# Seven inner products for each of three products: layer 1 of the last four batches of an attention and feed-forward kernel

## The chip, the cores and the metric

The kernel runs on one core of a Trainium2 chip. The metric is the device time of one execution in microseconds (us); lower is better. The engines are named as the profile names them: PE is TensorE's matmul, PEld its weight load, DVE is VectorE, ACT is ScalarE, POOL is GpSimd, and SP is the engine that issues most DMAs.

## What is computed

Eight batches of eight heads go through an attention whose queries are averaged in pairs: `softmax(scale * q_pool @ k.T) @ v`. This gives `x`, 576 rows of 512 numbers for each batch. Then, per batch, 128 rows are chosen by a gate score and only these pass a two-layer network:

```python
scores = np.einsum('bsd,d->bs', x, w_gate)
top_idx = np.argpartition(-scores[b], capacity)[:capacity]   # capacity 128
xe = x[b, top_idx]
h = np.maximum(xe @ w1, 0.0)                                 # w1 512 x 1024
ye = h @ w2                                                  # w2 1024 x 512
g = 1.0 / (1.0 + np.exp(-scores[b, top_idx]))
out[b, top_idx] = x[b, top_idx] + g[:, None] * ye
```

All of it is float32. The change concerns `xe @ w1` for batches 4 to 7 and the order of the work around it.

## The kernel before

The attention fills the first 568 us. It runs pair of heads by pair of heads, two batch halves in flight, with every matmul on 64 x 64 quarters of the array. Routing (choosing the 128 rows of a batch) is a Python generator that is advanced a piece at a time between the other work.

`ending` (L1381) then does the network for all eight batches, four at a time. The 128 chosen rows of four batches are 512 rows, and each of the two matrix products is made as a 2 x 2 block product in seven block products instead of eight. For layer 1 the four input blocks are named a11, a12, a21, a22 (two batches by half of the 512 inputs each), the weight blocks b11 to b22 (half of the inputs by half of the 1024 hidden units), and there are four sums of inputs s1 to s4 (`input_sums`, L1249, on POOL) and of weights t1 to t4 (made earlier, in the tile `tw`). `first_layer` (L1300) makes the products in the order a11 b11, a12 b21, s2 t2, s1 t1, s4 b22, s3 t3, a22 t4, which the text calls P1, P2, P4, P3, P6, P5 and P7. Each is a `first_product` (L1265): eight matmuls of a 128 x 128 weight block against 256 columns; each shows as two records in the profile. ACT copies the first to SBUF (`u`), and DVE adds the others onto running sums, 128 x 1024 at a time (L1298 is the shared helper `add`). When a hidden quarter c11, c12, c22 or c21 is complete, ACT applies the ReLU in place (L1309).

Layer 2 is the same scheme for two batches at a time. `second_of` (L1353) makes seven `second_product`s (L1280) of four matmuls with 256 columns each, in the order 1, 2, 7, 3, 4, 5, 6; ACT copies four of them and DVE adds the rest, then scales by the gate and adds to `xe` (L1293). Its input sums are `four_sums` (L1344) on DVE. `scattered` writes the finished rows back with an indirect DMA from POOL (L1240). The two last batches go through a layer 2 written out at the end of `ending`.

So the stages in time are: layer 1 of batches 0 to 3, layer 2 of batches 0 and 1, of 2 and 3, layer 1 of batches 4 to 7, layer 2 of 4 and 5, of 6 and 7. Between the products stand two other pieces of work: the routing of batches 6 and 7, advanced by `pieces` (L1389) at fixed counts (the tuple `behind`), and a check that no softmax sum is out of range: `counted` (L1505, two DVE passes over 576 columns into the tile `low`) and `outside` (L1522, one tiny matmul on `low` and three tiny DVE operations). In the kernel before these two stand after two and after four products of the second layer 1.

The schedule is manual: each engine executes its instructions in the order in which the program emits them. Every matmul result goes to a tile from `banks` (L1063); the pool has four tiles of two banks each, so that a product waits for a tile until its last reader on DVE or ACT is done.

Of the kernel before, what the change touches and what calls it, by code (L numbers as in the profile page):

```python
# [540 lines left out]
class _Plain:  # L541
# [704 lines left out]
            oob_is_err=False,  # L1246
        )

    def input_sums(self, a, s):  # L1249

        a11, a12, a21, a22 = a
        s1, s2, s3, s4 = s
        add, subtract = ALU.add, ALU.subtract
        for to, x, y, op in (
            (s1, a21, a22, add), (s2, s1, a11, subtract), (s3, a11, a21, subtract), (s4, a12, s2, subtract)
        ):
            self.nc.gpsimd.tensor_tensor(out=to, in0=x, in1=y, op=op)  # L1257

    def lines_of(self, room):
        return room.rearrange("p (c n) -> p c n", n=P)  # L1260
# [36 lines left out]
    def add(self, to, x, y):  # L1297
        self.nc.vector.tensor_tensor(out=to, in0=x, in1=y, op=ALU.add)  # L1298
# [54 lines left out]
    def second_of(self, tokens, a, s, y):  # L1353

        copy, add = self.nc.scalar.copy, self.add
        half, w = self.Dm // 2, tokens[0]["w"]
        y1, y2, y7, y3, y4 = (y[0:w, i * half : (i + 1) * half] for i in range(5))
        to = [token["xe"][0:w, i * half : (i + 1) * half] for token in tokens for i in range(2)]
        one, two = tokens
        products = self.second_layer(a, s, (1, 2, 7, 3, 4, 5, 6))  # L1360
        for part in (y1, y2, y7):
            copy(part, next(products))
            yield
        copy(y3, next(products))
        add(y2, y2, y1)
        self.scaled(to[0], y2, one, to[0])
        yield
        add(y4, y1, next(products))
        add(y3, y3, y4)
        add(y4, y4, y7)  # L1370
        yield
        ps = next(products)
        add(y4, y4, ps)
        add(y7, y3, ps)
        yield
        add(y3, y3, next(products))
        for of, at, token in ((y3, to[1], one), (y4, to[2], two), (y7, to[3], two)):
            self.scaled(at, of, token, at)
        yield

    def ending(self, halves, old):  # L1381

        nc, half, copy = self.nc, self.Dm // 2, self.nc.scalar.copy
        last = halves[-1]["pair"]
        w = self.tokens[0]["w"]
        n = self.NFC // 2 * 2 * P
        done, behind = 2, (3, 4, 5, 9, 10, 11, 12, 13, 18, 19, 21, 22, 27)

        def pieces(unit, n=None, of=1):  # L1389
            nonlocal done  # L1390
            for i, _ in enumerate(unit):
                for _ in range(of):
                    if done in behind:
                        next(waiting)
                    done += 1
                if i + 1 == n:
                    break

        def exponents_room():
            return self.row(self.work.tile([P, self.NG, G, 2, self.HALF], F32, name="p"))  # L1400

        def values_room():
            return self.row(self.load.tile([P, 2, self.NC, self.D], F32, name="v_sb", bufs=2))

        def sums_room():
            return self.row(self.work.tile([P, G, 2 * self.HALF], F32, name="acc"))

        def first(i):
            x, y = (self.tokens[4 * i + 2 * j]["turned"] for j in range(2))
            a = [t[:, :, k * self.ND // 2 : (k + 1) * self.ND // 2, 0:w] for t in (x, y) for k in range(2)]  # L1410
            c = [self.hidden_of(rooms[i][:, k * n : (k + 1) * n], w) for k in range(4)]
            m = [self.hidden_of(room[:, 4 * n : 5 * n], w) for room in rooms]
            return a, c, self.first_layer(a, inputs, c, m)

        def second(i, j, c):
            a = [c[2 * j + k][:, :, t, :] for t in range(2) for k in range(2)]
            s = self.lines_in(rooms[1 - i][:, 2 * j * n : 2 * (j + 1) * n], self.NFC // 2, w, 4)
            return self.tokens[4 * i + 2 * j : 4 * i + 2 * j + 2], a, s

        self.early = values_room()[:, 0 : 2 * self.Dm]  # L1420
        rooms, acc = [exponents_room()], [sums_room(), sums_room()]
        inputs = [acc[0][:, i * 2 * half : (i + 1) * 2 * half] for i in range(3)]
        inputs.append(self.load.tile([P, self.S], F32, name="kT")[:, 0 : 2 * half])
        inputs = [room.rearrange("p (t c n) -> p t c n", t=2, n=P)[:, :, :, 0:w] for room in inputs]

        self.gated(halves[-3])
        next(old)
        self.weighted(halves[-1])
        self.drained(halves[-1])
        self.multiplied(halves[-2])  # L1430
        rooms.append(exponents_room())
        a, c, layer = first(0)
        self.input_sums(a, inputs)
        self.multiplied(halves[-1])
        self.scored(halves[-3])
        self.gated(halves[-2])
        self.late = values_room()
        next(old)
        next(layer)
        self.normalized(last)  # L1440
        self.gated(halves[-1])
        self.scored(halves[-1])
        _, new, _ = self.routing.pop()
# [12 lines left out]
        self.scattered(x[0])  # L1456
        pieces(self.second_of(*y, acc[1]))
        a, c, layer = first(1)
        self.input_sums(a, inputs)
        self.scattered(y[0])  # L1460

        pieces(layer, 2)
        low = self.counted()
        pieces(layer, 2)
        outside = self.outside(low)
        pieces(layer, 1)
        x, y = second(1, 0, c), second(1, 1, c)
        self.four_sums(*x[1:])
        pieces(layer)
        layer = self.second_of(*x, acc[1])  # L1470
        pieces(layer, 3)
        self.four_sums(*y[1:])
        pieces(layer)
        self.scattered(x[0])

        (six, seven), c, s = y
        to = [token["xe"][0:w, i * half : (i + 1) * half] for token in (six, seven) for i in range(2)]
        y1, y3, y4 = (acc[1][0:w, i * half : (i + 1) * half] for i in range(3))
        found = nc.values_load(outside[0:1, 0:1])
        E = mybir.EngineType  # L1480
        self.tc.mark_branch_hint_location("again", found, [E.PE, E.DVE, E.Pool, E.Activation, E.SP])
# [212 lines left out]
```

## Time and profile before

| what | us |
|---|---|
| median of three runs (672.95 to 673.77) | 673.27 |
| the profiled execution's own time | 673.65 |
| its span in the profile | 671.9 |
| PE busy | 665.1 (99%) |
| DVE busy | 565.2 (84%) |
| POOL busy | 499.8 (74%) |
| ACT busy | 441.2 (66%) |
| layer 1 of batches 4 to 7 on PE | 617.40 to 641.89 |
| layer 2 of batches 4 and 5 on PE | 641.89 to 653.97 |

The span begins with the first instruction of the program that was recorded and ends with the last; the time of the same execution is 1.75 us longer. A group's line gives busy time and the mean duration of one instruction; on DVE and ACT durations of neighbours overlap by some 80 ns, so the step from one start to the next is shorter than a duration. A timeline line gives the start in us, the time until the last of its merged instructions ended, and how many there were.

### The profile page before, as it was taken

What the parts mean: (1) busy time and instruction counts of PE and PEld (TensorE: products, weight loads), DVE (VectorE), ACT (ScalarE), POOL (GpSimd) and SP (SyncE); (2) the same over time, 40 slices, a digit from 0 to 9 for tenths busy, and PEclk for the clock granted to TensorE, in tenths of its full rate; (3) what the DMA queues carried; (4) which work ended last, traced back from release to release, by engine and by line L of the source; (5) the groups of instructions that cost most, each with busy time, mean ns of one, the idle gap of its engine ahead of it and who ended that gap; (6) DMA issues with size and microseconds to landing.
All of it is one profiled execution on the core that took longest, in us unless ns stands there. A gap on an engine that the chain in (4) does not pass through costs nothing.

```text
span 671.9 us, 22869 instructions
## 1 busy us (share of the span) xinstructions
PE 665.1 (99%) x9715; PEld 438.4 (65%) x9715; DVE 565.2 (84%) x811; ACT 441.2 (66%) x959; POOL 499.8 (74%) x465
## 2 busy tenths in 40 slices
PE   9999999999999999999999999999999999999996
PEld 6656666666666666666666666656666666888885
DVE  3878999998999987998899888988898899596463
ACT  5677778777777777778777777777777874221120
POOL 5788888889888988899888978898889877302302
PEclk9999999999999999999999999999999999999999
DMA  8989989868886788859866879588958845303001
GB/s 164 169 178 194 216 173 189 150 113 179 159 154 117 122 163 153 166 105 177 170 117 130 170 137 149 127 160 146 156 112 163 153 139 151 73 16 105 33 2 66
DMA packets 391048, 92.68 MB, mean 138 GB/s; under 512 B 371608, under 2 KB 376088, under 8 KB 390936
## 3 DMA queue, kind: packets, MB, share of 16 engines
q1 hardware_dynamic: 389496, 86.73, 67.1%
q0 software_dynamic: 1280, 4.20, 1.7%
q8 instruction: 78, 1.28, 0.8%
q14 instruction: 34, 0.28, 0.2%
q10 hardware_dynamic: 160, 0.20, 0.1%
HBM read 75.30 MB, written 15.79 MB: 136 GB/s over the span
## 4 chain that ended last, share of the span: by engine, by line
PE 92%; issue 5%; DMA 2%; POOL 1%; DVE 0%; POOLq 0%
PE ps L878 42%; PE ps L896 42%; PE ps L1285 4%; PE ps L1271 4%; DMA out_dram<-xe,index 1%; PE ps L623 1%; DMA out_dram<-v_sb,index 0%; POOL acc L1257 0%; POOL out_dram L1240 0%; PE ps L844 0%; DVE xe L1293 0%; POOL kT L1257 0%; DVE v_sb L1215 0%; PE ps L830 0%; DVE acc L1298 0%
## 5 line engine op out<-in xcount | busy, mean ns | idle before, releaser
L885 ACT ACTIVATE p<-ps 128x576 f32<-128x576 f32 x576 | 320.5, 699 | 2.2 <-PE ps L878 1.9
L917 POOL TENSOR_TENSOR acc<-p 128x576 f32<-128x576 f32 x192 | 283.0, 1501 | 38.3 <-ACT p L885 36.9
L878 PE MATMUL ps<-qT,kT 64*64 64x288 f32 x4608 | 292.0, 403 | 0.0
L896 PE MATMUL ps<-p,v_sb 64*64 64x288 f32 x4608 | 290.9, 403 | 0.0
L878 PEld LDWEIGHTS ps<-qT,kT 64*64 64x64 f32 x4608 | 174.1, 133 | 105.5 <-ACT p L885 13.4
L896 PEld LDWEIGHTS ps<-p,v_sb 64*64 64x64 f32 x4608 | 173.0, 133 | 106.6 <-ACT p L885 14.7
L922 DVE TRANSPOSE_TENSOR_REDUCE fold<-p 128x54 f32<-128x1728 f32 x64 | 126.3, 1974 | 44.3 <-ACT p L885 44.2
L904 ACT COPY two<-ps 128x576 f32<-128x576 f32 x64 | 40.8, 638 | 133.5 <-PE ps L896 131.6
L922 DVE TRANSPOSE_TENSOR_REDUCE fold<-acc 128x54 f32<-128x1728 f32 x64 | 124.5, 1945 | 3.7 <-POOL acc L917 3.5
L906 POOL TENSOR_TENSOR av<-two 128x288 f32<-128x288 f32 x64 | 51.3, 801 | 39.9 <-ACT two L904 39.0
L766 DVE STREAM_TRANSPOSE kT<-kb 128x1152 f32<-128x1152 f32 x31 | 73.9, 2385 | 0.0
L985 POOL TENSOR_TENSOR prod<-avb,w_gate 128x288 f32<-128x288 f32 x64 | 51.5, 805 | 0.0
L1116 DVE TENSOR_SCALAR_CACHE_REDUCE pick<-line 128x127 f32<-128x127 f32 (+4 forms) x80 | 45.2, 564 | 3.4 <-DMA line<-gate_lines 1.2
L763 POOL TENSOR_TENSOR qp<-qb 128x576 f32<-128x576 f32 (+1 forms) x32 | 43.9, 1373 | 5.5 <-DMA qb<-in_q_dram 3.9
L962 ACT ACTIVATE sums<-total,tiny 32x18 f32<-32x18 f32 x124 | 38.2, 308 | 1.9
L1240 POOL DMA_INDIRECT out_dram<-xe,index x7 | 6.9, 992 | 38.7 <-DVE xe L1293 28.2
L1021 POOL TENSOR_TENSOR x<-avb,rec 128x576 f32<-128x576 f32 x30 | 34.8, 1161 | 0.0
L1309 ACT ACTIVATE p<-p 128x1024 f32<-128x1024 f32 x8 | 8.5, 1058 | 39.0 <-DVE p L1298 33.5
L975 DVE STREAM_TRANSPOSE avb<-av 128x288 f32<-128x288 f32 x64 | 28.3, 442 | 3.8 <-POOL av L906 3.8
L1043 DVE TENSOR_REDUCE red<-prod 128x9 f32<-128x288 f32 x64 | 27.8, 435 | 2.7 <-POOL prod L985 2.7
L947 ACT COPY groups<-sum 32x36 f32<-32x36 f32 x124 | 27.2, 219 | 1.6
L1298 DVE TENSOR_TENSOR p<-p,ps 128x1024 f32<-128x1024 f32 x14 | 16.9, 1216 | 11.9 <-PE ps L1271 11.8
(103 smaller groups left out, 420.7 us busy)
## 6 DMA issues: line engine op xcount, KB each, us to landing
kb<-in_k_dram SPq DMA_DIRECT2D x124, 144.0 KB, 4.7
qb<-in_q_dram SPq DMA_DIRECT2D x124, 144.0 KB, 4.5
v_sb<-in_v_dram SPq DMA_DIRECT2D x31, 576.0 KB, 5.1
out_dram<-x SPq DMA_DIRECT2D x128, 72.0 KB, 5.0
lines<-row_rank SPq DMA_DIRECT2D x8, 640.0 KB, 4.2
w<-in_moe_w_dram SPq DMA_DIRECT2D x8, 512.0 KB, 4.7
line<-gate_lines SPq DMA_DIRECT2D x8, 351.5 KB
tw<-tw SPq DMA_DIRECT2D x4, 512.0 KB, 5.7
```

The source lines that it names most:

```text
L763: nc.gpsimd.tensor_tensor(out=qp[:, of, :], in0=pair["q"][:, of, 0, :], in1=pair["q"][:, of, 1, :], op=ALU.add)
L766: nc.vector.transpose(kT.rearrange("p (c i g) -> p c g i", c=self.NC, i=BLK), pair["k"].rearrange("p (g c) d -> p c g d", c=self.NC),)
L878: nc.tensor.matmul(sc[keys, j, 0:n], lhsT=pair["kT"][rows, c * P + keys.start : c * P + keys.stop], rhs=pair["qT"][rows, qs], start=True, ...
L885: nc.scalar.activation(p[:, c // G, c % G, :, :], sc[:, :, 0:n], AF.Exp, scale=self.scale)
L896: nc.tensor.matmul(av[j * self.D : (j + 1) * self.D, e, 0:n], lhsT=half["pair"]["v"][keys, j, c, :], rhs=half["p"][keys, c // G, c % G, j, :],
L904: nc.scalar.copy(two[:, :, :], av[:, :, 0:n])
L906: nc.gpsimd.tensor_tensor(out=half["av"][:, :], in0=two[:, 0, :], in1=two[:, 1, :], op=ALU.add)
L917: nc.gpsimd.tensor_tensor(out=acc[:, u, :], in0=units[:, 0, u, :], in1=units[:, 1, u, :], op=ALU.add)
L922: nc.vector.tensor_reduce(fold[:, a, :], of.rearrange("p u (m d) -> p (u m) d", d=BLK), AX.X, ALU.add, apply_transpose=True,)
L962: self.nc.scalar.activation(tot[rows, :], pair["total"][:, j * self.QB : (j + 1) * self.QB], AF.Identity, bias=self.tiny[0:BLK, 0:1],)
L985: self.nc.gpsimd.tensor_tensor(out=pair["prod"][:, ns, :], in0=pair["avb"][:, ns, :], in1=self.w_gate[:, hp : hp + 1, :].broadcast_to([P, ...
L1116: nc.vector.tensor_scalar(out=cmp[0:rows, 0 : part.stop - part.start], in0=near[0:rows, part], scalar1=sc[0:rows, t : t + 1], scalar2=None ...
```

## The change

Four things are changed.

First, in layer 1 of batches 4 to 7 three of the seven products (P2, P6 and P7) are no longer eight matmuls over 256 columns. Each is divided once more into 2 x 2 blocks: the two batches of a block are taken singly (128 columns each), the contraction is split into its two 128-row chunks, the 512 hidden units into two times 256. An inner product is two matmuls of a 128 x 128 weight block against 128 columns, and seven of them replace the eight matmuls. They lie in halves of six banks (three tiles, taken together). ACT copies the first, and DVE makes seven adds of 128 x 256. P2's result is made in `c11` and P1 is added to it afterwards (`rest`); P6 is made in `u`; P7 is made in `c21`; then `rest` adds `u` to `c12` and `v` to `c21`.

Second, the inner sums are made on POOL: twelve weight sums of 128 x 256 (`inner_weights`, two at each step of `pieces` from the first layer 1 on, into six rooms that the attention leaves), and for each of the three products four input sums of 128 x 128 (`inner_inputs`).

Third, the ReLU of c22, c12 and c21 moves behind P7. The order of layer 2 in `second_of` becomes 1, 5, 2, 7, 3, 4, 6 with other accumulators, in all three calls of it.

Fourth, `counted` and `outside` move into the layer 2 of batches 4 and 5: `counted` after its third product, `outside` after its fourth. The first input sum that layer 2 needs is made between P6 and P5, the other three after P7, and the scatter of batches 2 and 3 is emitted after layer 1.

```diff
+    def inner_weights(self, operands):
+        rooms = self.quarter_rooms()
+        n = self.F // 4
+        for operand in operands:
...
+            for i in range(4):
...
+                self.nc.gpsimd.tensor_tensor(out=to, in0=x, in1=y, op=ALU.subtract)
+                t.append(to)
+                yield
+
+    def inner_product(self, tile, k, i, of, by):
+        to = tile[:, k, 2 * i * P : 2 * (i + 1) * P].rearrange("p (f n) -> p f n", n=P)[:, :, 0 : of.shape[1]]
+        for f in range(2):
+            self.nc.tensor.matmul(to[:, f, :], lhsT=by[:, f * P : (f + 1) * P], rhs=of, start=True, stop=True)
+        return to
+
+    def inner_layer(self, m, to, temps):
...
+        x, y, z = self.banks(), self.banks(), self.banks()
+        u, v, r = temps
+        self.nc.scalar.copy(u, product(x, 0, 0, a11, b11))
+        add(r, u, product(x, 1, 0, s2, t2))
+        add(c11, u, product(y, 0, 0, a12, b21))
+        add(v, r, product(y, 1, 0, s1, t1))
+        ps = product(z, 0, 0, s3, t3)
+        add(c22, v, ps)
+        add(r, r, ps)
+        add(c12, v, product(z, 1, 0, s4, b22))
+        add(c21, r, product(x, 0, 1, a22, t4))
...
+            def layer():
+                copy(across(u), product(a[0], self.quarter(1, 0, 0)))
+                yield
+                self.inner_layer(two, c11, temps[0])
+                rest(c11, u)
+                relu(c11)
+                yield
+                add(across(v), across(u), product(s2, t2))
+                yield
+                add(across(c12), across(v), product(s1, t1))
+                yield
+                self.inner_layer(six, u, temps[1])
+                self.four_sums(*x[1:], slice(2, 3))
+                yield
+                ps = product(s3, t3)
+                add(across(v), across(v), ps)
+                add(across(c22), across(c12), ps)
+                yield
+                self.inner_layer(seven, c21, temps[0])
+                relu(c22)
+                rest(c12, u)
+                relu(c12)
+                rest(c21, v)
+                relu(c21)
+                yield
...
-        products = self.second_layer(a, s, (1, 2, 7, 3, 4, 5, 6))
-        for part in (y1, y2, y7):
-            copy(part, next(products))
-            yield
-        copy(y3, next(products))
-        add(y2, y2, y1)
+        products = self.second_layer(a, s, (1, 5, 2, 7, 3, 4, 6))
+        copy(y1, next(products))
+        yield
+        copy(y5, next(products))
+        yield
+        add(y2, y1, next(products))
         self.scaled(to[0], y2, one, to[0])
         yield
+        add(y2, y5, next(products))
+        yield
+        copy(y3, next(products))
+        yield
         add(y4, y1, next(products))
+        add(y2, y2, y4)
         add(y3, y3, y4)
-        add(y4, y4, y7)
-        yield
-        ps = next(products)
-        add(y4, y4, ps)
-        add(y7, y3, ps)
+        add(y5, y5, y3)
...
+                    for _ in range(2):
+                        next(weights, None)
...
+        self.inner_inputs(operands[0])
         pieces(self.second_of(*y, acc[1]))
-        a, c, layer = first(1)
         self.input_sums(a, inputs)
+        for operand in operands[1:]:
+            self.inner_inputs(operand)
+        c, x, layer = split(a)
+        pieces(layer)
+        self.four_sums(*x[1:], slice(0, 2))
+        self.four_sums(*x[1:], slice(3, 4))
         self.scattered(y[0])
-
-        pieces(layer, 2)
-        low = self.counted()
-        pieces(layer, 2)
-        outside = self.outside(low)
-        pieces(layer, 1)
-        x, y = second(1, 0, c), second(1, 1, c)
-        self.four_sums(*x[1:])
-        pieces(layer)
+        y = second(1, 1, c)
         layer = self.second_of(*x, acc[1])
         pieces(layer, 3)
+        low = self.counted()
+        pieces(layer, 1)
+        outside = self.outside(low)
         self.four_sums(*y[1:])
         pieces(layer)
         self.scattered(x[0])
```

More of the change, by code (lines that the diff above doesn't have):

```diff
@@ L1247, in written, with input_sums @@
         )
-    def input_sums(self, a, s):
+    def input_sums(self, a, s, which=slice(0, 4)):
         a11, a12, a21, a22 = a
@@ L1253, in input_sums, with quarter_rooms @@
         add, subtract = ALU.add, ALU.subtract
-        for to, x, y, op in (
-            (s1, a21, a22, add), (s2, s1, a11, subtract), (s3, a11, a21, subtract), (s4, a12, s2, subtract)
-        ):
+        steps = (s1, a21, a22, add), (s2, s1, a11, subtract), (s3, a11, a21, subtract), (s4, a12, s2, subtract)
+        for to, x, y, op in steps[which]:
             self.nc.gpsimd.tensor_tensor(out=to, in0=x, in1=y, op=op)
+    def quarter_rooms(self):
+        load, work = self.load, self.work
+        yield load.tile([P, self.QB, BLK], F32, name="qp", bufs=1)
+        for _ in range(2):
+            yield load.tile([P, self.Sp], F32, name="qT")
+        yield work.tile([P, self.QB, BLK], F32, name="prod", bufs=1)
+        for name in ("avb", "avb"):
+            yield work.tile([P, self.QB, BLK], F32, name=name)
@@ new lines, in inner_weights @@
+    def inner_weights(self, operands):
+        rooms = self.quarter_rooms()
+        n = self.F // 4
+        for operand in operands:
+            t = operand["t"] = []
+            b11, b12, b21, b22 = (operand["b"][:, k, j * n : (j + 1) * n] for k in range(2) for j in range(2))
+            for i in range(4):
+                if i % 2 == 0:
+                    room = next(rooms)
+                    room = self.row(room) if len(room.shape) > 2 else room
+                to = room[:, i % 2 * n : (i % 2 + 1) * n]
+                x, y = ((b12, b11), (b22, t[0] if t else None), (b22, b12), (b21, t[1] if i == 3 else None))[i]
+                self.nc.gpsimd.tensor_tensor(out=to, in0=x, in1=y, op=ALU.subtract)
+                t.append(to)
+                yield
@@ new lines, in inner_inputs @@
+    def inner_inputs(self, operand):
+        room, w = operand["room"], operand["a"].shape[3]
+        a = [operand["a"][:, i, j, :] for i in range(2) for j in range(2)]
+        operand["s"] = [room[:, i * P : i * P + w] for i in range(4)]
+        self.input_sums(a, operand["s"])
+    def inner_product(self, tile, k, i, of, by):
[3 more added lines that the diff above has]
+        return to
@@ new lines, in inner_layer @@
+    def inner_layer(self, m, to, temps):
+        n = self.F // 4
+        product, add = self.inner_product, self.add
+        a11, a12, _, a22 = (m["a"][:, k, j, :] for k in range(2) for j in range(2))
+        b11, _, b21, b22 = (m["b"][:, k, j * n : (j + 1) * n] for k in range(2) for j in range(2))
+        (s1, s2, s3, s4), (t1, t2, t3, t4) = m["s"], m["t"]
+        c11, c12, c21, c22 = (to[:, 2 * i : 2 * i + 2, :] for i in range(4))
+        x, y, z = self.banks(), self.banks(), self.banks()
[9 more added lines that the diff above has]
+        add(c21, r, product(x, 0, 1, a22, t4))
@@ L1356, in second_of @@
         half, w = self.Dm // 2, tokens[0]["w"]
-        y1, y2, y7, y3, y4 = (y[0:w, i * half : (i + 1) * half] for i in range(5))
+        y1, y2, y5, y3, y4 = (y[0:w, i * half : (i + 1) * half] for i in range(5))
         to = [token["xe"][0:w, i * half : (i + 1) * half] for token in tokens for i in range(2)]
         one, two = tokens
-        products = self.second_layer(a, s, (1, 2, 7, 3, 4, 5, 6))
-        for part in (y1, y2, y7):
-            copy(part, next(products))
-            yield
-        copy(y3, next(products))
-        add(y2, y2, y1)
+        products = self.second_layer(a, s, (1, 5, 2, 7, 3, 4, 6))
[4 more added lines that the diff above has]
+        add(y2, y1, next(products))
         self.scaled(to[0], y2, one, to[0])
         yield
+        add(y2, y5, next(products))
+        yield
+        copy(y3, next(products))
+        yield
         add(y4, y1, next(products))
+        add(y2, y2, y4)
         add(y3, y3, y4)
-        add(y4, y4, y7)
-        yield
-        ps = next(products)
-        add(y4, y4, ps)
-        add(y7, y3, ps)
+        add(y5, y5, y3)
         yield
         add(y3, y3, next(products))
-        for of, at, token in ((y3, to[1], one), (y4, to[2], two), (y7, to[3], two)):
+        for of, at, token in ((y3, to[1], one), (y2, to[2], two), (y5, to[3], two)):
             self.scaled(at, of, token, at)
@@ L1394, in pieces @@
                         next(waiting)
+                    for _ in range(2):
+                        next(weights, None)
                     done += 1
@@ L1406, in sums_room, with halves_of @@
             return self.row(self.work.tile([P, G, 2 * self.HALF], F32, name="acc"))
[L1408 to L1411, printed above, removed]
+        def halves_of(turned):
+            k = self.ND // 2
+            return turned[:, :, 0:k, 0:w], turned[:, :, k:, 0:w]
@@ L1412, in first, with lines, across @@
+        def first():
+            a = [half_of for token in self.tokens[0 : self.B // 2 : 2] for half_of in halves_of(token["turned"])]
+            c = [self.hidden_of(rooms[0][:, k * n : (k + 1) * n], w) for k in range(4)]
             m = [self.hidden_of(room[:, 4 * n : 5 * n], w) for room in rooms]
             return a, c, self.first_layer(a, inputs, c, m)
+        def lines(room):
+            return self.lines_of(room)[:, :, 0:w]
+        def across(room):
+            return room.rearrange("p (t f) n -> p f t n", t=2)
@@ new lines, in rest, with relu, split @@
+        def rest(to, x):
+            self.add(to, to, x)
+        def relu(to):
+            nc.scalar.activation(to, to, AF.Relu)
+        def split(a):
+            u, v = (lines(room[:, 4 * n : 5 * n]) for room in rooms)
+            c11, c12, c21, c22 = c = [lines(rooms[1][:, k * n : (k + 1) * n]) for k in range(4)]
+            temps = [
+                [lines(rooms[0][:, k : k + half]) for k in range(2 * n + 3 * i * half, 2 * n + 3 * (i + 1) * half, half)]
+                for i in range(2)
+            ]
+            two, six, seven = operands
+            s1, s2, s3, s4 = inputs
+            t1, t2, t3, _ = (self.summed(1, i) for i in range(4))
+            x, product, add = second(1, 0, c), self.first_product, self.add
+            def layer():
[23 more added lines that the diff above has]
+                yield
+            return c, x, layer()
@@ L1415, in second @@
         def second(i, j, c):
-            a = [c[2 * j + k][:, :, t, :] for t in range(2) for k in range(2)]
+            if i == 0:
+                a = [c[2 * j + k][:, :, t, :] for t in range(2) for k in range(2)]
+            else:
+                a = [c[2 * j + k][:, 4 * t : 4 * t + 4, :] for t in range(2) for k in range(2)]
             s = self.lines_in(rooms[1 - i][:, 2 * j * n : 2 * (j + 1) * n], self.NFC // 2, w, 4)
@@ L1431, in ending @@
         rooms.append(exponents_room())
-        a, c, layer = first(0)
+        a, c, layer = first()
         self.input_sums(a, inputs)
@@ L1442, in ending @@
         self.scored(halves[-1])
+        operands = [
+            {"b": b, "room": rooms[0][:, k * n // 2 : (k + 1) * n // 2]}
+            for b, k in ((self.quarter(1, 1, 0), 1), (self.quarter(1, 1, 1), 2), (self.summed(1, 3), 3))
+        ]
+        weights = self.inner_weights(operands)
         _, new, _ = self.routing.pop()
@@ L1456, in ending @@
         self.scattered(x[0])
+        a = [half_of for token in self.tokens[self.B // 2 :: 2] for half_of in halves_of(token["turned"])]
+        for operand, of in zip(operands, (a[1], inputs[3], a[3])):
+            operand["a"] = of
+        self.inner_inputs(operands[0])
         pieces(self.second_of(*y, acc[1]))
-        a, c, layer = first(1)
         self.input_sums(a, inputs)
-        self.scattered(y[0])
-        pieces(layer, 2)
-        low = self.counted()
-        pieces(layer, 2)
-        outside = self.outside(low)
-        pieces(layer, 1)
-        x, y = second(1, 0, c), second(1, 1, c)
-        self.four_sums(*x[1:])
-        pieces(layer)
+        for operand in operands[1:]:
[4 more added lines that the diff above has]
+        self.four_sums(*x[1:], slice(3, 4))
+        self.scattered(y[0])
+        y = second(1, 1, c)
         layer = self.second_of(*x, acc[1])
         pieces(layer, 3)
+        low = self.counted()
+        pieces(layer, 1)
+        outside = self.outside(low)
         self.four_sums(*y[1:])
```

## The prediction

> **What bounds the kernel now.** I read the page first: its busy table and its chain of work.
>
> ```profile
> PE 665.1 (99%) x9715; PEld 438.4 (65%) x9715; DVE 565.2 (84%) x811; ACT 441.2 (66%) x959; POOL 499.8 (74%) x465
> PE 92%; issue 5%; DMA 2%; POOL 1%; DVE 0%; POOLq 0%
> ```
>
> TensorE is busy for 99% and the chain runs over it, so a change pays what it takes off PE, less every wait it puts in front of PE. The whole network takes only 100 us of PE, so next I read the timeline of PE from layer 1 of batches 4 to 7 on:
>
> ```profile
> 617.40 7.07 PE L1271 MATMUL ps<-xeT,w 128*128 128x256 f32 x32
> 624.30 7.07 PE L1271 MATMUL ps<-acc,tw 128*128 128x256 f32 x32
> 631.30 0.19 PE L1526 MATMUL ps<-low,ones 128*1 128x2 f32 x2
> ```
>
> Two products start 6.90 us apart, so one takes 3.45 us, and one of its 16 records 216 ns. There is no hole; only the tiny matmul of the range check costs some 0.3 us. Layer 2 of batches 4 and 5 begins at 641.89, 24.49 after 617.40; its products take 1.73 each (one starts at 645.34, the next at 647.07).
>
> Then I read when the other engines serve PE, in the timeline of all engines. These are their prices:
>
> ```profile
> 592.40 2.34 DVE L1298 TENSOR_TENSOR p<-p,ps 128x1024 f32<-128x1024 f32 x2
> 600.71 2.61 DVE L1351 TENSOR_TENSOR p<-p 128x512 f32<-128x512 f32 x4
> 608.34 1.27 DVE L1298 TENSOR_TENSOR acc<-acc,ps 128x256 f32<-128x256 f32 x3
> 621.05 1.01 ACT L1311 COPY p<-ps 128x1024 f32<-128x1024 f32 x1 [8.26 <-PE ps L1271]
> 641.31 1.06 ACT L1309 ACTIVATE p<-p 128x1024 f32<-128x1024 f32 x1 [3.82 <-DVE p L1298]
> 625.71 0.74 DVE L1511 TENSOR_SCALAR_CACHE_REDUCE pick<-sums 128x576 f32<-128x576 f32 x1
> 626.50 0.75 DVE L1511 TENSOR_SCALAR_CACHE_REDUCE pick<-sums 128x576 f32<-128x576 f32 x1
> ```
>
> An add over 1024 lasts 1.21 and the next starts 1.13 after it (2.34 less 1.21). An add over 256 lasts 0.41; the three of 1.27 start 0.33 and 0.52 apart, and the longer step is the one behind a result that it waited for. `counted` takes 1.55 with its read-outs. A ReLU takes 1.06.
>
> [...] two loads behind a short matmul start 0.11 apart, and three short matmuls on 128 columns end 0.11 apart with a load each:
>
> ```profile
> 571.98 0.19 PEld L998 LDWEIGHTS ps<-sum,merge 128*128 128x128 f32 x1
> 572.09 0.19 PEld L1271 LDWEIGHTS ps<-xeT,w 128*128 128x128 f32 x1
> ...
> 8.12 0.44 PE L844 MATMUL ps<-ident,p 128*128 128x128 f32 x2
> 8.12 0.55 PE L844 MATMUL ps<-ident,p 128*128 128x128 f32 x3
> ```
>
> [...] In the trace, too, the copies of layer 2 at 599.46 stand behind a ReLU that waited until 598.28, although their first products had ended at 594.65 and 596.38.
>
> **What is removed from PE.** Three products of 16 records, 3.45 each. In place of one come 7 x 2 matmuls, 28 records. A record of half the columns takes 108 ns (half of 216) if matmul-bound, 110 if load-bound; I take 108.5. So 28 x 0.1085 = 3.04, and a product saves 0.41: three save 1.24 us. The ends are 0 (at 123 ns a record) and 1.29.
>
> **What POOL gets.** Twelve weight sums of 256: by the rows of 288 (0.79) and 512 (1.27) some 0.75 each, 9 us in all. They start after POOL's last gate product at 576.65 and end by 586; POOL's next work came at 588.79, so routing doesn't wait. Without that cover each would delay batch 7's gate by 0.75. Input sums of 128 cost some 0.45: the four for P2 fit between the scatter that ends at 618.16 and `input_sums` at 620.53, and PE wants them at 620.85. The other eight follow s4 at 625.6 and end by 629.4, wanted at 630.8 and later. The scatter behind them is waited for by nothing until 655. Cost: nothing.
>
> **What the new order does to layer 2 of batches 0 to 3.** On DVE the search for batch 7's indices waits for a DMA until 606.88 and ends at 608.42. In the kernel before, the add that frees the fifth product's tile (604.09) came ahead of this search. Now products 4's and 6's adds come behind it, at 608.34, so that batches 2 and 3's third product, due at 608.76, finds its tile free at about 608.8, plus 0.11 for a first weight load that isn't hidden: 0.17 us lost. The copies of y1 and y5 wait behind the same adds, with slack. Bounds: 0 (another tile is given) and 0.55 (it waits for y1's copy). Routing of batch 7 keeps its times, since its search still waits for the DMA and its transpose at 619.25 stays the last of that layer.
>
> **Layer 1 of batches 4 to 7, step by step.** I lay the instructions out from its start T = 0, each at the later of its engine's turn and its input. A consumer starts 0.2 after its product's last issue slot ends.
>
> PE, without waits: P1 to 3.45, P2 to 6.49, P4 to 9.94, P3 to 13.40, P6 to 16.44, P5 to 19.89, P7 to 22.93. Tiles: at every point three are free in time, P5's being last (22.4 for 22.9).
>
> DVE keeps up until P5. P5's two adds of 1024 start at 20.09 and hold DVE until 22.35. P7's first inner result was ready at 20.96, but its adds stand behind. Seven adds, mostly at 0.33 and one at 0.52, take 2.5: until 24.85. `rest(c12, u)` ends at 26.06, its ReLU at 27.15. Layer 2's products 1 and 5 cover PE from 22.93 to 26.38; product 2 reads c12 and starts only at 27.2, with another 0.11 for the weight load: 0.93 lost.
>
> What is late next: `rest(c21, v)` to 27.2, then s1, s2, s4 at about 0.7 each to 29.3, the add for product 2 and a scaling to 30.1, and `counted` to 31.67. In the new order `outside`'s matmul stands in PE's queue behind product 7, which ends at 30.76, and ahead of product 3. It waits for `low` until 31.72: 0.96 lost. In the kernel before, `low` was ready at 627.3 for a matmul at 631.30; that cover of 4 us is gone. Everything later on PE is queued behind it. The matmul's own cost is as before.
>
> Sum: -1.24 + 0.17 + 0.93 + 0.96 = +0.82. As a check by place: three products of layer 2 were left at 648.79 before; now at 617.57 + 31.72 + 0.3 = 649.6, so +0.8. The rest (layer 2 of batches 6 and 7, last scatter) keeps its length. From the profiled execution (673.65, span 671.9) that is 674.45, span 672.7; the median of the runs is 0.38 lower, so I predict 673.27 + 0.8 = 674.1.
>
> **Rivals.**
>
> *VectorE chain as above (A).* For it: strict order, and the rows of DVE's prices. 674.1, own range 673.5 to 674.8; chance 0.5.
>
> *VectorE has it done in time (B).* If both waits vanish, the time is 673.27 - 1.24 + 0.1 = 672.1; if one stays, 673.1. For it: DVE is busy for only 13.7 of the 24.5 us of this layer, and my chain has 1.9 us to lose. Against it: the adds of P5 cannot start before P5 ends, and behind them 11.6 us of work precede `low`, where PE has 3.04 + 4 x 1.73 = 9.95. Chance 0.23.
>
> *VectorE's adds come slower (C), which ends slower.* The place is P7's seven adds. If each takes the 0.52 step, because it waits for its own engine's last result, they take 3.64 rather than 2.5 and `low` is 1.1 later: 675.2. It decides from +0.55 on that chain, an average step of 0.44. For it: the 0.52 step stands in the trace; against it: only one of the seven reads the result just ahead of it. Chance 0.19.
>
> *The change doesn't do what it says (D): half-length matmuls don't run at half the time.* If a record took the 190 ns that a weight load's row shows, P2, P6 and P7 would take 5.32 each, +5.6 in all; DVE would then catch up and most of the waits vanish: 679. From 123 ns on nothing is saved. Against it are the steps of 0.11 shown above. Chance 0.08, counting milder forms around 676.
>
> **How the numbers follow.** The point is A's. A and B with one wait left lie within 0.2% (1.35 us, about what a measurement of this kernel can tell from no change). Faster needs 671.9 or less, which is B with no wait and a bit more: 0.06. Slower needs 674.6 or more: C, D and a quarter of A's spread: 0.29. The rest, 0.65, is same. The range 672.3 to 675.7 takes in B's middle and C, and leaves out D and B's low end. Its bounds also hold the tile's 0 to 0.55[...].
>
> **What would show it.** In the changed profile: 128-column records with starts 0.11 apart and P2, P6 and P7 some 3.0 long (else D); a weight load at layer 2's third product that waits for ACT's ReLU, some 0.8; PE idle before `outside`'s matmul, some 1.0, released by DVE; `rest` and seven 256 adds in unbroken file after P5 on DVE, stepping by 0.33 (0.52 for C); a wait of 0.1 to 0.5 near 608.8. The prediction is wrong if PE waits in a place that I have down as free: for a tile inside an inner product, for POOL's input sums, or in the routing of batch 7.

## The result, and the profile after

The changed kernel takes 682.88 us (median of four runs, 682.64 to 683.13). The kernel before, run beside it, takes 673.11 (672.88 to 673.77). The ratio is 1.0144, with a 95% interval of 1.0126 to 1.0161. The change costs 9.8 us, where 0.8 was predicted, and the result lies outside the predicted range of 672.3 to 675.7.

The busy table and the chain of work, on the page of the changed kernel:

```profile
PE 665.9 (98%) x9751; PEld 438.9 (64%) x9751; DVE 574.5 (84%) x832; ACT 441.6 (65%) x959; POOL 516.2 (76%) x489
PE 90%; issue 5%; DMA 2%; POOL 1%; DVE 1%; POOLq 0%; ACT 0%; DVEq 0%
```

PE's busy time is only 0.8 us more than before, although the span has grown from 671.9 to 681.0. So PE doesn't work longer; it stands still. The waits view of PE from 616 us on (what waited, on what; total us, times, longest) says where:

```profile
PE ps L1296 <- DVE p L1358: 5.0, 6, 1.0
PE ps L1296 <- ACT p L1309: 1.2, 2, 0.6
PE ps L1296 <- POOL acc L1256: 1.0, 1, 1.0
PE ps L1656 <- DVE pick L1641: 0.9, 1, 0.9
```

L1296 is the matmul of `inner_product`, L1358 the helper `add`, L1309 the copy of the first inner result, and L1656 the matmul of `outside`. Nine waits lie inside the three divided products, 7.2 us in all, and had not been predicted; the tenth, before `outside`, had. The timeline of PE shows one divided product, P6, record by record:

```profile
633.70 0.61 PE L1296 MATMUL ps<-kT,w 128*128 128x128 f32 x4
634.86 0.68 PE L1296 MATMUL ps<-p,qT 128*128 128x128 f32 x4 [0.55 <-ACT p L1309]
635.38 0.61 PE L1296 MATMUL ps<-kT,w 128*128 128x128 f32 x4
636.50 0.71 PE L1296 MATMUL ps<-p,qT 128*128 128x128 f32 x4 [0.51 <-DVE p L1358]
637.05 0.61 PE L1296 MATMUL ps<-p,prod 128*128 128x128 f32 x4
638.67 0.68 PE L1296 MATMUL ps<-p,w 128*128 128x128 f32 x4 [1.01 <-DVE p L1358]
639.19 0.61 PE L1296 MATMUL ps<-kT,prod 128*128 128x128 f32 x4
639.64 3.62 PE L1331 MATMUL ps<-acc,tw 128*128 128x256 f32 x16
```

One line is one inner product (two matmuls, four records). Two of them with no wait between start 0.45 apart (639.19 to 639.64). The second, fourth and sixth each wait. These are the second results in a tile: the inner products lie in pairs, first and second in x, third and fourth in y, fifth and sixth in z, one to a bank. The same stretch on the readers' side, ACT and DVE:

```profile
634.34 0.37 ACT L1309 COPY p<-ps 128x256 f32<-128x256 f32 x1 [4.58 <-PE ps L1296]
...
635.65 0.80 DVE L1358 TENSOR_TENSOR p<-p,ps 128x256 f32<-128x256 f32 x2 [0.53 <-PE ps L1296]
...
637.25 1.27 DVE L1358 TENSOR_TENSOR p<-p,ps 128x256 f32<-128x256 f32 x3 [0.81 <-PE ps L1296]
```

The copy of the first result lasts from 634.34 to 634.71; the second inner product starts at 634.86, right behind it. DVE's two adds from 635.65 (of the second result and the third) end at 636.45; the fourth inner product starts at 636.50. PE writes, the reader reads, PE writes again, in turn. The longest wait is before the sixth, because the fifth result has two readers and DVE has the fourth's add in front of them: the three adds from 637.25 end at 638.52, and the sixth starts at 638.67. The one wait that the view puts down to POOL is P2's first, 1.02 until 622.01. The POOL sum that ends then, at 621.86, makes one of the 128 x 512 sums, which P2 doesn't read. At the same time, 621.86, ACT ends its copy of P2's first inner result, which had stood behind the long copy of P1 (timeline of ACT):

```profile
620.58 1.01 ACT L1506 COPY p<-ps 128x1024 f32<-128x1024 f32 x1 [6.53 <-PE ps L1331]
621.48 0.38 ACT L1309 COPY p<-ps 128x256 f32<-128x256 f32 x1
```

What the divided products cost follows from their starts. P6 takes 639.64 - 633.70 = 5.94. From the same timeline P2 takes 6.41 (620.38 to 626.79) and P7 6.40 (643.10 to 649.50). Together that is 18.75, against 3 x 3.45 = 10.35 for three whole products: 8.40 more. A restart costs more than the listed idle time: the first weight load then starts at most 0.04 ahead of its matmul (634.83 for 634.86 on PEld's timeline), where without a wait it starts 0.11 ahead (635.27 for 635.38), so that the next inner product starts 0.52 later (634.86 to 635.38), not 0.45, and some 0.16 pass that the wait's own figure leaves out (634.86 less 634.15, where PE would have gone on, is 0.71; the wait is listed as 0.55). Nine times some 0.24 is 2.2, and 7.2 + 2.2 = 9.4 us of waits, against 1.0 saved by the shorter matmuls.

The rest of the difference stands behind the divided products:

```profile
654.68 1.89 PE L1345 MATMUL ps<-kT,p 128*128 128x256 f32 x8
657.51 0.19 PE L1656 MATMUL ps<-low,ones 128*1 128x2 f32 x2 [0.94 <-DVE pick L1641]
```

The product before `outside` would have handed over at 654.68 + 1.73 = 656.41; the matmul came at 657.51, 1.10 later. So 8.40 + 1.10 = 9.5 us are lost from this layer 1 on. In the profiled execution it had begun 0.48 earlier than before (616.92 against 617.40), and the last group of PE starts at 671.55, 8.94 later than before. That agrees with the profiled executions' own times, 682.71 against 673.65; the medians lie 9.8 apart because the profiled execution of the kernel before was 0.5 above its median, and that of the changed kernel 0.2 below.

### The profile page after: what moved, and what is told of

Its sections match the earlier page's. It is cut to its first block, busy times and chain, and to the rows that moved or that the text cites. A ratio compares the mean times of both kernels' runs of the same rounds, so it can differ in the third digit from the quotient of the medians.

```text
span 681.0 us, 23010 instructions
## 1 busy us (share of the span) xinstructions
PE 665.9 (98%) x9751; PEld 438.9 (64%) x9751; DVE 574.5 (84%) x832; ACT 441.6 (65%) x959; POOL 516.2 (76%) x489
## 3 DMA queue, kind: packets, MB, share of 16 engines
q8 instruction: 78, 1.28, 0.8%
## 4 chain that ended last, share of the span: by engine, by line
PE 90%; issue 5%; DMA 2%; POOL 1%; DVE 1%; POOLq 0%; ACT 0%; DVEq 0%
PE ps L878 41%; PE ps L896 41%; PE ps L1331 4%; PE ps L1345 3%; DMA out_dram<-xe,index 1%; PE ps L623 1%; POOL p L1256 1%; DMA out_dram<-v_sb,index 0%; DVE acc L1358 0%; POOL out_dram L1240 0%; DVE xe L1353 0%; PE ps L1296 0%; POOL acc L1256 0%; POOL kT L1256 0%; DVE v_sb L1215 0%
## 5 line engine op out<-in xcount | busy, mean ns | idle before, releaser
L1358 DVE TENSOR_TENSOR p<-p,ps 128x256 f32<-128x256 f32 (+1 forms) x32 | 21.5, 692 | 16.7 <-PE ps L1331 8.5
L771 DVE STREAM_TRANSPOSE qT<-qp 128x576 f32<-128x576 f32 (+1 forms) x32 | 23.4, 731 | 0.7 <-POOL qp L763 0.7
```

## The experiments

**The question.** The theory: a matmul that puts a second result into a tile is held until the first result in it has been read, although it writes to another bank; the emitted order (product, reader, product, reader) then makes PE and the readers take turns. Rivals: it is the bank that is held; DVE's seven adds and their hand-overs set the pace; it is the inputs from POOL that come late; a short matmul is simply slow; or the new order around it costs the time. Every kernel here computes all of the outputs. "Before beside it" is the kernel before, run in the same series.

**All seven matmul pairs ahead of the first reader.** The seventh result moves from x to z.

```diff
-        self.nc.scalar.copy(u, product(x, 0, 0, a11, b11))
-        add(r, u, product(x, 1, 0, s2, t2))
...
+        p1, p2 = product(x, 0, 0, a11, b11), product(x, 1, 0, s2, t2)
+        p3, p4 = product(y, 0, 0, a12, b21), product(y, 1, 0, s1, t1)
+        ps, p6 = product(z, 0, 0, s3, t3), product(z, 1, 0, s4, b22)
+        p7 = product(z, 0, 1, a22, t4)
+        self.nc.scalar.copy(u, p1)
+        add(r, u, p2)
...
```

> The changed kernel, but inside each divided product all seven inner products are issued before the first of their readers, and the seventh lies in the third tile; products, banks in number and sums are the same. Tile theory (a second result into a two-bank tile waits until the reader of the first one is done, though it lies in another bank): TensorE's waits inside the three divided products go, each takes 3.0 to 3.1 us instead of 6.4, 5.9 and 6.4, and about 0.9 comes back as the wait for c12's ReLU, so 674 us (673.3 to 675). VectorE theory (seven sums of 256 with a hand-over each set the pace): they stay near 5 us or more each, 679 or more.

Measured: 674.47, before beside it 673.52, ratio 1.0016 (1.0010 to 1.0023). Of the 9.8 us, 8.8 are gone. P6 on the timeline of PE, and what comes after:

```profile
630.62 0.61 PE L1296 MATMUL ps<-kT,w 128*128 128x128 f32 x4
631.06 0.61 PE L1296 MATMUL ps<-p,qT 128*128 128x128 f32 x4
...
633.30 0.61 PE L1296 MATMUL ps<-kT,prod 128*128 128x128 f32 x4
633.74 3.62 PE L1334 MATMUL ps<-acc,tw 128*128 128x256 f32 x16
...
642.05 1.89 PE L1348 MATMUL ps<-kb,p 128*128 128x256 f32 x8
644.54 1.99 PE L1348 MATMUL ps<-w,p 128*128 128x256 f32 x8 [0.60 <-ACT p L1494]
...
649.20 0.19 PE L1659 MATMUL ps<-low,ones 128*1 128x2 f32 x2 [0.94 <-DVE pick L1644]
```

P6 takes 633.74 - 630.62 = 3.12. The bodies, the operands and the POOL sums are those of the change; only the order of emission and the place of the seventh result differ. So neither short matmuls nor POOL's inputs nor the pace of DVE's seven adds hold PE. The readers, too, seem to wait for the tile: ACT's copy of P6's first result starts 0.20 after the second inner product has handed over (631.71 after 631.51), where in the changed kernel it starts 0.19 after the first (634.34 after 634.15). And with these waits gone, the two that the prediction did forecast appear: the third product of this layer 2 starts at 644.54 instead of 642.05 + 1.73 = 643.78, 0.76 late behind the ReLU of c12 (and its next product another 0.1), and `outside` 1.1 late.

**Both results of a tile in one bank.** The pairs keep their order and their tiles, but lie in the halves of one bank.

```diff
-        add(r, u, product(x, 1, 0, s2, t2))
+        add(r, u, product(x, 0, 1, s2, t2))
...
-        add(v, r, product(y, 1, 0, s1, t1))
+        add(v, r, product(y, 0, 1, s1, t1))
...
-        add(c12, v, product(z, 1, 0, s4, b22))
-        add(c21, r, product(x, 0, 1, a22, t4))
+        add(c12, v, product(z, 0, 1, s4, b22))
+        add(c21, r, product(x, 1, 0, a22, t4))
```

> The changed kernel, with the two results of a tile put into the two halves of one bank, so that six of the seven results lie in three banks rather than six. Tile theory: the wait is already there for the other bank, so nothing changes: within 0.4 of 682.9. A theory in which the six banks do buy overlap between TensorE and the readers: slower by 1 us or more.

Measured: 683.19, before beside it 673.52, ratio 1.0146 (1.0124 to 1.0168). P6's three waits on the timeline of PE:

```profile
635.21 0.68 PE L1296 MATMUL ps<-p,qT 128*128 128x128 f32 x4 [0.55 <-ACT p L1309]
...
636.85 0.71 PE L1296 MATMUL ps<-p,qT 128*128 128x128 f32 x4 [0.51 <-DVE p L1358]
...
639.02 0.68 PE L1296 MATMUL ps<-p,w 128*128 128x128 f32 x4 [1.01 <-DVE p L1358]
```

They are those of the change, to the hundredth. Lying in the same bank or in two makes no difference to these waits, so it is not the bank that is held.

**Successive results in different tiles.** The order of emission is that of the change, but the tiles go round: x, y, z, x, y, z, x.

```diff
-        add(r, u, product(x, 1, 0, s2, t2))
-        add(c11, u, product(y, 0, 0, a12, b21))
-        add(v, r, product(y, 1, 0, s1, t1))
-        ps = product(z, 0, 0, s3, t3)
+        add(r, u, product(y, 0, 0, s2, t2))
+        add(c11, u, product(z, 0, 0, a12, b21))
+        add(v, r, product(x, 1, 0, s1, t1))
+        ps = product(y, 1, 0, s3, t3)
```

> The changed kernel with the inner results in the order tile 1, 2, 3, 1, 2, 3, 1, so that the reader that has to be done is three products back and not one. Tile theory: P2 and P6 lose their waits but for some tenths, P7 keeps one wait of about 1.1 behind the two long adds of P5: 675 us (674 to 677). VectorE theory: 679 or more.

Measured: 675.52, before beside it 673.52, ratio 1.0028 (1.0017 to 1.0039). A second visit to a tile now comes three inner products later, and mostly its reader is done. Against 3.12 without a wait P2 loses 0.4 and P6 0.2 (3.50 and 3.32 from start to start); P7 keeps one wait, at its fifth inner product, because its readers stand behind the two long adds of P5 (on DVE, in one file from 637.54 to 640.89):

```profile
638.68 0.61 PE L1296 MATMUL ps<-p,avb 128*128 128x128 f32 x4
640.37 0.68 PE L1296 MATMUL ps<-p,avb 128*128 128x128 f32 x4 [1.08 <-DVE p L1358]
```

The three experiments together settle the mechanism: moving readers behind the writes removes the waits, moving a result within the tile does not, moving it to another tile does for as long as DVE keeps up.

**Three whole products, everything else as changed.** Each divided product becomes a whole one with a copy by ACT; the new order, POOL's inner sums (now unused) and the late check stay.

```diff
-                self.inner_layer(two, c11, temps[0])
+                copy(across(c11), product(a[1], self.quarter(1, 1, 0)))
...
-                self.inner_layer(six, u, temps[1])
+                copy(across(u), product(inputs[3], self.quarter(1, 1, 1)))
...
-                self.inner_layer(seven, c21, temps[0])
+                copy(across(c21), product(a[3], self.summed(1, 3)))
```

> The changed kernel with its new order, late ReLUs, moved range check and GpSimd's inner sums, but P2, P6 and P7 made as whole products and copied by ScalarE. Tile theory: the loss lies in the divided products alone, 673.0 to 674.0. Rest theory (the new order, the late ReLUs or the moved check lose the time): 678 or more.

Measured: 674.56, before beside it 673.52, ratio 1.0015 (1.0008 to 1.0022). All of the order's cost is 1.0 us, and the trace has one wait from 608 us on for it, before `outside`:

```profile
646.07 1.89 PE L1345 MATMUL ps<-kT,p 128*128 128x256 f32 x8
648.89 0.19 PE L1656 MATMUL ps<-low,ones 128*1 128x2 f32 x2 [0.93 <-DVE pick L1641]
```

**P6 alone divided.** As the last, but with P6 left as in the change.

```diff
-                self.inner_layer(two, c11, temps[0])
+                copy(across(c11), product(a[1], self.quarter(1, 1, 0)))
...
-                self.inner_layer(seven, c21, temps[0])
+                copy(across(c21), product(a[3], self.summed(1, 3)))
```

> The changed kernel with P6 alone divided, as the change does it, P2 and P7 whole with a copy by ScalarE. Tile theory: each divided product pays its own waits, so P6 adds 5.94 less 3.45, 2.5 us, to the kernel with three whole products: 677.0 (676.5 to 677.6). If the waits came from VectorE's backlog over several divided products, one alone would cost less than 1.

Measured: 676.48, before beside it 673.18, ratio 1.0048 (1.0033 to 1.0063). Against three whole products this is 3.30 - 1.04 = 2.3 more; from the changed kernel's trace, P6 costs 5.94 - 3.45 = 2.5 more. The loss goes by the divided product.

**The check moved early, on the change and on the version with the writes first.** `counted` comes after P1 and `outside` after P4, as early as in the kernel before.

```diff
         c, x, layer = split(a)
+        pieces(layer, 1)
+        low = self.counted()
+        pieces(layer, 2)
+        outside = self.outside(low)
         pieces(layer)
...
-        pieces(layer, 3)
-        low = self.counted()
-        pieces(layer, 1)
-        outside = self.outside(low)
+        pieces(layer, 4)
```

On the change alone:

> The changed kernel with its readers as they are, and only the range check moved to after P1 and P4. It takes the 1.1 us of that wait: 681.8 (681.3 to 682.4). If the moved check were the loss, it would come near 674.

Measured: 681.38, before beside it 673.18, ratio 1.0122 (1.0107 to 1.0138). The wait before `outside` is gone, the nine others remain; the cost falls from 9.8 to 8.2. The first of the nine, which the changed kernel's waits view puts down to POOL, is here put down to ACT's copy like those of P6 and P7.

With the writes first as well:

> Results issued ahead of their readers, and only the range check moved to after P1 and P4; c12's ReLU stays behind P7. The wait of 1.1 in front of the check's matmul goes, the wait for c12's ReLU of 0.8 stays: 673.4 (673.0 to 674.0).

Measured: 673.07, before beside it 673.18, ratio 0.9998 (0.9990 to 1.0007). One wait is left in these stages, 0.6 us behind the ReLU of c12.

**An attempt on that last wait, which missed.** Besides the last edits, `rest` and the ReLU of c12 come ahead of P7's adds.

```diff
                 add(across(c22), across(c12), ps)
+                rest(c12, u)
+                relu(c12)
                 yield
...
                 relu(c22)
-                rest(c12, u)
-                relu(c12)
```

> Results issued ahead of their readers, and the two waits of layer 2 taken away as well: the two passes of the range check stand after P1 and its small matmul after P4, and the last sum and the ReLU of c12 stand ahead of P7. Tile theory with the prediction's chain for the rest: TensorE doesn't wait in these stages, so three divided products save 0.33 each against the kernel before: 1.0 us under it, 672.5 (672.0 to 673.1). If the sums of P7, now one long add later, hold up layer 2 instead: about the time before, 673.5.

Measured: 673.10, before beside it 673.18, ratio 0.9999 (0.9991 to 1.0007). It was expected at 672.5. One line each from the timelines of ACT, DVE and PE shows why:

```profile
641.49 0.35 ACT L1313 COPY p<-ps 128x256 f32<-128x256 f32 x1
...
641.88 2.60 DVE L1361 TENSOR_TENSOR p<-p,ps 128x256 f32<-128x256 f32 x7 [1.38 <-ACT p L1313]
...
642.35 1.99 PE L1348 MATMUL ps<-kb,p 128*128 128x256 f32 x8 [0.65 <-DVE p L1361]
```

The copy of P7's first result now stands in ACT's queue behind the ReLU. It comes at 641.49, DVE idles 1.38 for it, the adds empty P7's tiles later, and layer 2's second product waits 0.65 for a tile. A wait for data had become a wait for room. (The seven adds step by some 0.37 here: 2.60 less 0.41, over six.)

**The sum for c12 on POOL.** POOL has nothing to do there, and the copy keeps its place ahead of the ReLU.

```diff
                 add(across(c22), across(c12), ps)
+                nc.gpsimd.tensor_tensor(out=c12, in0=c12, in1=u, op=ALU.add)
                 yield
                 self.inner_layer(seven, c21, temps[0])
+                relu(c12)
                 relu(c22)
-                rest(c12, u)
-                relu(c12)
```

> As the kernel with results ahead of their readers and the early range check, but the last sum of c12 is made by GpSimd, idle at that place, ahead of P7, and c12's ReLU is the first behind the copy of P7's first result. VectorE then begins P7's seven adds 1.1 us earlier than with c12's sum in front, and no ReLU stands in front of P7's copy. TensorE should not wait at the start of layer 2 at all (0.8 before): 1.0 us under the kernel before, 672.2 to 672.6 where that is 673.3. If VectorE's chain behind P5 still holds a tile or c12 late: no faster than 673.0.

Measured: 672.81, before beside it 673.60, ratio 0.9986 (0.9980 to 0.9993). This is 0.8 us under the kernel before, with the interval clear of 1, so it beats both kernels, if by little. The timelines of POOL and PE:

```profile
640.61 2.37 POOL L1525 TENSOR_TENSOR p<-p 128x1024 f32<-128x1024 f32 x1 [9.89 <-DVE p L1361]
...
641.03 1.89 PE L1348 MATMUL ps<-w,p 128*128 128x256 f32 x8
642.76 1.89 PE L1348 MATMUL ps<-kb,p 128*128 128x256 f32 x8
644.49 1.89 PE L1348 MATMUL ps<-w,p 128*128 128x256 f32 x8
```

Layer 2's first three products start 1.73 apart, and PE waits for nothing in these stages. On PE layer 1 takes 23.51 us (617.52 to 641.03), where it took 24.49. So the divided products pay what their matmuls save, about 1 us, once their waits and those of the order are gone.

## Why the prediction was wrong, step by step

**The step that failed** reads: "Tiles: at every point three are free in time, P5's being last (22.4 for 22.9)." It asked whether three whole tiles are free when a divided product begins. They are: no first inner product waits. It didn't ask what holds *inside* a product, where each tile takes two results and the first is read before the second is emitted. The text named "for a tile inside an inner product" among the places that would make it wrong, but gave it no price and no rival. It could have been bounded from the code and the rows shown. The diff emits a reader between the two writes of each tile, which is visible. If the second write waits, each pair runs as matmuls, hand-over, read. The prediction's own 0.2 from product to consumer and 0.41 for an add make some 0.6 per pair, three pairs to a product: nine waits of 0.61, some 5.5 us, on the slower side. That would have been a rival worth stating.

| term | predicted, us | changed kernel, us |
|---|---|---|
| shorter matmuls, three products | -1.24 | -0.96 |
| waits inside the three products | 0 | +9.4 |
| third product of layer 2, batches 2 and 3 | +0.17 | 0 |
| third product of layer 2, batches 4 and 5, for c12 | +0.93 | 0 |
| before `outside` | +0.96 | +1.10 |

*The records.* A record of 128 columns was put at 108.5 ns and takes 112 (639.19 to 639.64 is four), a little over even the 110 that the prediction read from steps of 0.11. 28 x 0.112 = 3.14, and P6 took 3.12 with the writes first, so that some 0.32 is saved and not 0.41. That such records run at about half time, against rival D, was right: 112 ns, where one of 256 columns takes 216.

*POOL's sums* at no cost: right, though not all took the 0.45 of the estimate (those for P2 took 0.48 to 0.63, the first for P7 1.48). The experiment with the writes first has no wait for any of them.

*The first half.* No wait came near 608.8. The step had taken the search's DMA as fixed at 606.88. In the changed kernel the search starts sooner and the product is on time (timelines of DVE and PE):

```profile
605.63 1.35 DVE L1152 SCALAR_TENSOR_TENSOR pick<-lines,token,token_line 128x640 f32<-128x640 f32 x1 [1.59 <-DMA lines<-row_rank]
...
608.29 1.89 PE L1345 MATMUL ps<-w,p 128*128 128x256 f32 x8
```

Of these 1.25 us some 0.47 are DVE's, which came to the search's first DMA earlier (SP issues it at 600.35, before at 600.82). Between this issue and that of the second DMA, which reads back what the first wrote, pass 1.45 us instead of 2.32; why is not known. The whole of layer 2 for batches 0 to 3 took 24.24 on PE, and 24.48 before; the experiments, with the same code there, took 24.24 to 24.66, so that nothing can be read from this difference.

*The waits behind P7.* For c12 none came in the changed kernel: PE was itself late in P7 by more than DVE (P7 took 6.40, and 3.12 with the writes first). Rival D's remark, that DVE then catches up, holds here for another cause. With the writes first the chain is there: DVE's two long adds and seven short ones were put at 2.26 + 2.5, and took 4.86 in one file:

```profile
637.40 4.86 DVE L1361 TENSOR_TENSOR p<-p,ps 128x1024 f32<-128x1024 f32 x9 [1.44 <-PE ps L1334]
```

The ReLU wait was 0.87 for 0.93 and `outside`'s 1.1 for 0.96, and that kernel's loss of 0.95 stands beside the predicted 0.8. Rival B (all in time) and rival C (adds at 0.52 throughout) are both out on that run. So this part of the working holds for a kernel which differs from the changed one only in the order in which PE's writes and their readers are emitted, and in the tile of each product's seventh result.

*What stays open.* Writes first avoids the wait by order. Whether the wait could simply be dropped where the two results lie in different banks wasn't tried. For banks of different tiles the runs show PE writing one bank while ACT reads another: with the writes first, ACT reads P6's x from 631.71 to 632.08, while PE writes y from 631.51 on, its inner products still 0.45 apart (631.51 to 631.96; timeline of ACT):

```profile
631.71 0.37 ACT L1313 COPY p<-ps 128x256 f32<-128x256 f32 x1 [3.64 <-PE ps L1296]
```

For two banks of one tile no run here shows it, because the program waits for the tile in every case.

## What to carry to other kernels

When a result is split into parts of one buffer, list for each part the write, its reader, and the next write to the same buffer in emitted order: if a reader stands between two writes and the program guards the buffer as a whole, as it did here, price that hand-over as a wait (0.5 to 1.0 us each here) on the engine that sets the time, whichever bank the parts lie in. Issuing all the writes first, or sending successive results to different buffers, cost 1.0 and 2.0 us against the kernel before here, where the interleaved order cost 9.8. When a wait is taken away, look at what else shares the queues of the moved instructions: the early ReLU only turned a wait for data into one for room, and the idle engine was the better place.

## What was unexpected of the hardware

DVE and POOL took longer in places where both worked from SBUF at the same time. Three scalings with two SBUF operands took 1.28 us in the kernel before and 1.83 beside POOL's new sums of 128 x 128 (617.49 to 619.77). In the version with the writes first, a DVE sum of 128 x 1024 from SBUF took 1.61, where the shortest such sum is 1.22, and POOL's small sum beside it 1.31, where the next took 0.46 (timelines of DVE and POOL; the first line is the kernel before's, the second the changed kernel's):

```profile
618.05 1.28 DVE L1293 SCALAR_TENSOR_TENSOR xe<-acc,own_gate,xe 128x256 f32<-128x256 f32 x3
```

```profile
617.63 1.83 DVE L1353 SCALAR_TENSOR_TENSOR xe<-acc,own_gate,xe 128x256 f32<-128x256 f32 x3
```

```profile
625.36 1.61 DVE L1361 TENSOR_TENSOR p<-p 128x1024 f32<-128x1024 f32 x1
...
624.62 1.28 POOL L1256 TENSOR_TENSOR kT<-xeT,acc 128x512 f32<-128x512 f32 x1
625.97 1.31 POOL L1256 TENSOR_TENSOR p<-kT 128x128 f32<-128x128 f32 x1
627.37 0.46 POOL L1256 TENSOR_TENSOR p<-p,kT 128x128 f32<-128x128 f32 x1
```

DVE's sum started while POOL's larger one was still at work (until 625.90). The small sum ended at 627.28, 0.3 after DVE's; in the changed kernel one took 1.48 (from 627.51) beside a DVE sum of 1.23 (from 627.45), and ended 0.3 after DVE's as well. What makes them longer is not shown: no run here was made to tell. The prediction's prices for POOL (0.45 for 128 x 128) were taken from rows with no such neighbour. It cost nothing here, since POOL's sums had cover.
